# Attention and feed-forward on one core: batch 0's token transpose placed ahead of batch 1's query transpose, and the third w2 block sum moved to VectorE

## Chip, cores and metric

The kernel runs on one core of one Trainium2 chip, in one launch. The metric is the device time of that launch in microseconds (us). Five runs of the kernel before gave 280.51 to 281.52 us, with a median of 280.81 us. One further execution was profiled.

## What is computed

There are 8 batches, 8 heads, 576 positions and 64 features per head. The first half is an attention that never forms a 576 x 576 matrix; the second half is a layer norm and a feed-forward block with a residual:

```
q_s = softmax of q over the 64 features;  k_s = softmax of k over the 576 positions
kv  = einsum('bhsd,bhse->bhde', k_s, v);  attn = einsum('bhsd,bhde->bhse', q_s, kv)
x   = attn as (batch, 576, 512)
out = x + relu(layer_norm(x, g_ln, eps=1e-6) @ w_ch1) @ w_ch2      # w_ch1 512 x 2048, w_ch2 2048 x 512
```

Inputs and output are float32.

## The kernel before

**Tiling.** Of each batch, 512 positions are handled as four tiles of 128; the last 64 positions of all eight batches are collected into a ninth group (`xT8`, `x8`). For every batch the attention result is made with features on the partitions (`xsT`, 128 x 512 in four slices). This is what the first matmul reads. The residual, the statistics of the layer norm and the final additions need it the other way round, with positions on the partitions (`x`). That copy is made by a DMA transpose, `x<-xsT` at L487 in `tokens()`. Four BATCH_NORM_STATS2 (L490) and four aggregates (L491) on VectorE then give the variances, and two small ScalarE operations (L492, L494) the reciprocal deviation `rstd`. Centring is folded into the weights (`centre_w1`), so the first matmul does not wait for the statistics; only the last additions (`ot`, `cp`) do.

**Attention of a batch.** The loads of q, k and v go into staging buffers `stg` (L239, all on SP's queue). ScalarE takes the exponential of q (L326); VectorE sums it (`zq`, L328), takes the reciprocal (`rzq`, L330) and scales (`eq`, L332). A DMA transpose (`eqT<-eq`, L337, in `dma_t()`) turns the scaled queries. ScalarE makes `ek` (L353) and `vb` (L359) from k and v; TensorE forms the 64 x 64 products per head (L370), and VectorE and ScalarE scale them to `kve`. Then TensorE forms `xT` from `eqT` and `kve` (L398; L421 for the last 64 positions), and ScalarE copies it to `xsT` (L411).

**Feed-forward of a batch.** `mm1` runs 16 groups of four matmuls (L538, 128x512), each group evicted with a ReLU to `hT` (L501 on ScalarE; for batch 0 some on VectorE, L503). Batch 0 then uses the plain `mm2` (L681, 64 matmuls of 128x512 into the four `pg` banks). Its four results are evicted at L694, which reads `pg`, `rstd` and `x`. Batches 1 to 7 and the ninth group use `mm2_split`, a product of 2 x 2 blocks with seven block products (L618). It needs sums of blocks of `hT` (`S`, L554) and of `w2` (`T`, L569, made once in `w2_sums`), and evicts through L628. Of the four sums T0 to T3 in `w2_sums`, T2 runs on GpSimd, the others on VectorE; each is made in four pieces of 128x512. The GpSimd pieces read a one-column tile `hold` that GpSimd copies from batch 0's first result `ot` (L754), so they start after it.

**What sets the order.** All work is first entered in a `Plan` as tasks: engine, estimated duration, class, reads, writes, tasks it must follow in order (`after`), and a `slack` that is added to the moment at which it counts as ready. `order()` simulates the engines with these numbers. Whenever an engine is free it takes, of the ready tasks, the one of the lowest class and then of the lowest number. DMAs share one modelled queue; a DMA transpose is entered with 0.9 MB and a landing time, and keeps SP until 0.8 us before its data have passed the queue. `emit()` writes the instructions in that order, so each engine runs a fixed list. When a wait takes longer on the chip than in the plan, everything behind it on that engine waits too.

**Around the change.** Loads are chained through `gate[1]` in the order in which they are entered. The first batch whose attention overlaps feed-forward work is batch 1 (`kind == "early"`). At the end of its loads, after the last load of v, the code enters the query transpose and then the tokens of batch 0:

```
            gate[1] = dma_t()
            state["eqT"] = gate[1], tokens(0, 0.7, (gate[1],))
```

Batch 2's loads follow `state["eqT"]`. Inside `mm2(0)`, the `xT` matmuls of batch 1 may enter TensorE's list after chosen steps (`second_x`, L687). Batch 1's `mm1` reads `xsT` of batch 1, and its first four groups write `pa` banks; the fifth group is the first that needs a `pg` bank released by L694.

Of the kernel before, what the change touches and what calls it, by code (L numbers as in the profile page):

```python
# [12 lines left out]
FP32 = mybir.dt.float32  # L13
# [4 lines left out]
ALU = mybir.AluOpType  # L18
# [116 lines left out]
def dve_t(n, mode=1):  # L135
    return 0.15 + n / (960.0 * mode)
# [3 lines left out]
def kernel(  # L140
# [10 lines left out]
    nc = tc.nc  # L151
# [3 lines left out]
    P = 128  # L155
    J = 4
# [13 lines left out]
    def sb(shape, dt, name):  # L170
        return persist.tile(shape, dt, name=name, tag=name)
# [12 lines left out]
    eq = [sb([P, 2, JT, P], BF16, f"eq{i}") for i in range(2)]  # L184
    eqT = [sb([P, 2 * JT, P], BF16, f"eqT{i}") for i in range(2)]
    kve = [sb([P, G, D], FP16, f"kve{i}") for i in range(2)]
    hold = sb([P, 1], FP32, "hold")
    xb = [sb([P, J, DM], FP16, f"x{i}") for i in range(3)]
    x8 = sb([P, J, DM], FP16, "x8")
    xsT = [sb([P, J * KO1, P], FP16, f"xsT{i}") for i in range(2)]  # L190
# [3 lines left out]
    ot = [sb([P, 2, DM], FP32, f"ot{i}") for i in range(NOT)]  # L194
# [5 lines left out]
    T = [sb([P, HK, 256], FP16, f"T{i}") for i in range(4)]  # L200
# [3 lines left out]
    bst = sb([P, J, 6], FP32, "bst")  # L204
# [6 lines left out]
    plan = Plan()  # L211
# [3 lines left out]
    def nxt(what, n):  # L215
        i = cnt[what] % n
        cnt[what] += 1
        return i
# [17 lines left out]
    gate = [(), None]  # L236
# [72 lines left out]
    def attn(b, kind, between=None, exps=(), sums_=(), kvs=()):  # L309
# [5 lines left out]
        cls = 0 if kind == "first" else 1  # L315
# [20 lines left out]
        def dma_t():  # L336
            return plan.add("SP", 2.2, lambda: nc.sync.dma_start_transpose(  # L337
                eqT[u], eq[u].rearrange("p q j c -> p (q j c)")),
                r=[("eq", u, 0), ("eq", u, 1)], w=EK(u), mb=0.9, land=3.5 if steady else 0.6, after=() if steady else (gate[1],))
# [122 lines left out]
        if steady:  # L462
            state["eqT"] = (dma_t(),)
        else:
            gate[1] = dma_t()
            state["eqT"] = gate[1], tokens(0, 0.7, (gate[1],))
        for hf in range(2):
            keys(hf, lk[hf])
            values(hf, lv[hf])
# [7 lines left out]
    def xof(c):  # L477
        return (xb[c % 3], ("x", c % 3), st[c % 3], ("st", c % 3)) if c < B else (x8, "x8", st[3], ("st", 3))

    def tokens(c, cls=1, after=(), stats=()):  # L480

        x, xk, sti, stk = xof(c)
        if c < B:
            src, r = xsT[c % 2], XK(c % 2)
        else:
            src, r = xT8, [("xT8", b, i) for b in range(B) for i in range(2)]
        i = plan.add("SP", 2.2, lambda: nc.sync.dma_start_transpose(x.rearrange("p j (k c) -> p (j k) c", k=KO1), src.rearrange("p n t -> p (n t)")),  # L487
                 r=r, w=[(xk, j) for j in range(J)], mb=0.9, land=0.6, after=after)
        for j in range(J):
            plan.add("DVE", dve_t(512), lambda j=j: nc.vector.bn_stats(bst[:, j, :], x[:, j, :]), r=[(xk, j)], w=[("bst", j)], cls=cls, slack=2.0 if c else 0.5, after=stats)  # L490
            plan.add("DVE", 0.18, lambda j=j: nc.vector.bn_aggr(bmv[:, j, :], bst[:, j, :]), r=[("bst", j)], w=[("bmv", j)], cls=cls)  # L491
        plan.add("ACT", 0.3, lambda: nc.scalar.activation(sti[:, 3, :], bmv[:, :, 1], AF.Ln, bias=eps, scale=GS * GS),  # L492
                 r=["eps"] + [("bmv", j) for j in range(J)], w=[(stk, "v", j) for j in range(J)], cls=0)
        state["rstd"] = plan.add("ACT", 0.2, lambda: nc.scalar.activation(sti[:, 4, :], sti[:, 3, :], AF.Exp, scale=-0.5),  # L494
                 r=[(stk, "v", j) for j in range(J)], w=[(stk, "r", j) for j in range(J)], cls=0)
        return i


# [58 lines left out]
        tt(3, h12, S[1][:, ks], ALU.subtract, sk(1) + hi)  # L557
        tt(2, h11, h21, ALU.subtract, lo)

    def w2_sums(k0, n, after):  # L560

        ks, kh = slice(k0, k0 + n), slice(HK + k0, HK + k0 + n)
        b11, b12 = w2_sb[:, ks, 0:256], w2_sb[:, ks, 256:512]
        b21, b22 = w2_sb[:, kh, 0:256], w2_sb[:, kh, 256:512]
        lo, hi = [("w2", k0 + i) for i in range(n)], [("w2", HK + k0 + i) for i in range(n)]
        tk = lambda i: [("T", i, k0 + j) for j in range(n)]
        def tt(i, a, b, r):
            eng, e = ("POOL", nc.gpsimd) if i == 2 else ("DVE", nc.vector)
            plan.add(eng, 1.2 if i == 2 else dve_t(256 * n, 2), lambda: e.tensor_tensor(T[i][:, ks], a, b, op=ALU.subtract),  # L569
                     r=r + (["hold"] if i == 2 else []), w=tk(i), cls=2, after=after if i == 2 else ())  # L570
        tt(0, b12, b11, lo)
        tt(1, b22, T[0][:, ks], hi + tk(0))
        tt(2, b22, b12, lo + hi)
        tt(3, b21, T[1][:, ks], hi + tk(1))
# [5 lines left out]
    def store(c, o, hf):  # L580

        if c == B:
            plan.add("SP", 0.62, lambda: nc.sync.dma_start(last_rows(hf), ot[o]), r=[("ot", o, 0), ("ot", o, 1)], mb=0.52, land=2.0, cls=0)
            return
        for e in range(2):
            src = ot[o][R * e : R * e + R]
            plan.add("SP", 0.62, lambda e=e, src=src: nc.sync.dma_start(
                out[c].rearrange("(p j) c -> p j c", j=JT)[:, 4 * hf + e : 4 * hf + e + 3 : 2, :], src),
                r=[("ot", o, 0), ("ot", o, 1)], mb=0.36, land=2.0, cls=0)
# [82 lines left out]
    def mm2(c):  # L672

        gis = [nxt("pg", 4) for _ in range(J)]
        ids = []
        steps = [(8, 1), (8, 3), (12, 1)]
        for k0 in range(0, KO2, 4):
            for j in range(J):
                def f(k0=k0, j=j):
                    for kk in range(k0, k0 + 4):  # L680
                        nc.tensor.matmul(pg[gis[j]], hT[:, kk, j * P : j * P + P], w2_sb[:, kk, :],  # L681
                                         start=(kk == 0), stop=(kk == KO2 - 1))
                i = plan.add("PE", 0.864, f, r=[("hT", kk) for kk in range(k0, k0 + 4)] + [("w2", kk) for kk in range(k0, k0 + 4)], w=[("pg", gis[j])])
                if j == 0:
                    ids.append(i)
                if (k0, j) in steps:
                    second_x(steps.index((k0, j)), (i,))  # L687
        plan.fill(ids[0], ids[-1], zeros(pg[gis[0]], False))
        evs = []
        for hf in range(2):  # L690
            o = nxt("ot", NOT)
            for i in range(2):
                j = 2 * hf + i
                ev = plan.add("DVE", dve_t(512), lambda o=o, i=i, j=j: nc.vector.scalar_tensor_tensor(  # L694
                    ot[o][:, i, :], in0=pg[gis[j]], scalar=st[c % 3][:, 4, j : j + 1], in1=xb[c % 3][:, j, :],
                    op0=ALU.mult, op1=ALU.add),
                    r=[("pg", gis[j]), (("x", c % 3), j), (("st", c % 3), "r", j)], w=[("ot", o, i)], cls=0)
                evs.append(ev)
            store(c, o, hf)
        return evs[:1]  # L700

    def zeros(bank_, start):
        def f(n):
            for _ in range(n):
                nc.tensor.matmul(bank_, zero[:, :P], zero, start=start, stop=start, skip_group_check=True)  # L705
        return f
# [7 lines left out]
    state = {"eqT": (), "ev": [], "stats": ()}  # L714
    opened = [nxt("pg", 4) for _ in range(4)]
    open_ids = []
    def first_w1():
        centre_w1(0)
        open_ids.extend(mm1_open(opened))

    rest = attn(0, "first", first_w1)
    for blk in range(1, 4):
        load_w1(blk)
# [11 lines left out]
    w2_rows(0)  # L735
    w2_rows(4)
    second_x = attn(1, "early", second_w2)

    before = ()
    for b in range(B):  # L740
        if b:
            state["tok"] = tokens(b, 0.7, stats=state["stats"])
        if b == B - 1:
            tokens(8, 0.7, stats=state["stats"])
        ids = mm1(b, b > 0, () if b else opened)
        if b == 0:
            plan.fill(warmed, open_ids[0], zeros(pg[3], True))
            plan.fill(open_ids[-1], ids[0], zeros(pg[opened[0]], False))
        elif b < B - 1:
            attn(b + 1, "steady", None, before, (ids[0],), (ids[10],))  # L750
        before = (ids[-1], state["rstd"])
        if b == 0:
            evs = mm2(b)
            plan.add("POOL", 0.2, lambda: nc.gpsimd.tensor_copy(hold, ot[0][:, 0, :1]), r=[("ot", 0, 0)], w=["hold"])  # L754
            for k0 in range(0, HK, 2):
                w2_sums(k0, 2, evs)
        else:
            mm2_split(b)
    mm1(8, True)
# [37 lines left out]
```

The softmax here doesn't subtract the row's maximum and nothing guards it: scores larger than these inputs give would overflow.

## Time and profile before

| what | value |
|---|---|
| median of five runs (lowest to highest) | 280.81 us (280.51 to 281.52) |
| the profiled execution, its own time | 280.94 us |
| its span in the profile | 279.2 us |
| granted TensorE clock | 1.00 |
| TensorE busy (matmuls) | 271.0 us, 97% of the span |
| VectorE / ScalarE / GpSimd busy | 199.1 / 167.6 / 5.9 us |
| share of the chain that ended last: TensorE, VectorE, DMA, ScalarE | 78%, 13%, 6%, 2% |
| DMA moved | 55.35 MB, mean 198 GB/s |

The profile lists for each group of instructions its line, engine, operation and tile, its busy time, and the idle time of the engine just ahead of it with what ended it. Matmul spans overlap, so a busy TensorE need not be at its peak; its idle stretches are what can be won back. The chain of work that ended last is followed back from the last instruction, at each step to what released it. From about 83.5 us to the last store that chain is almost wholly TensorE; before that it passes through VectorE, DMA and ScalarE as well.

### The profile page before, as it was taken

What the parts mean: (1) busy time and instruction counts of PE and PEld (TensorE: products, weight loads), DVE (VectorE), ACT (ScalarE), POOL (GpSimd) and SP (SyncE); (2) the same over time, 40 slices, a digit from 0 to 9 for tenths busy, and PEclk for the clock granted to TensorE, in tenths of its full rate; (3) what the DMA queues carried; (4) which work ended last, traced back from release to release, by engine and by line L of the source; (5) the groups of instructions that cost most, each with busy time, mean ns of one, the idle gap of its engine ahead of it and who ended that gap; (6) DMA issues with size and microseconds to landing.
All of it is one profiled execution on the core that took longest, in us unless ns stands there. A gap on an engine that the chain in (4) does not pass through costs nothing.

```text
span 279.2 us, 5657 instructions
## 1 busy us (share of the span) xinstructions
PE 271.0 (97%) x2327; PEld 164.5 (59%) x2327; DVE 199.1 (71%) x406; ACT 167.6 (60%) x273; POOL 5.9 (2%) x15
## 2 busy tenths in 40 slices
PE   8999999989799999999999999999999999999994
PEld 2444444436674478447844784478447844874583
DVE  0878896499859967976599569764996773641572
ACT  4668976399468695668566946685655077016500
POOL 1000000060000000000000000000000000000000
PEclk9999999999999999999999999999999999999999
DMA  7999999998977996579858975798543450023004
GB/s 261 363 386 387 387 389 192 270 347 228 337 245 150 220 382 71 150 163 384 124 151 164 392 116 150 160 391 122 153 85 72 81 153 0 0 49 104 0 2 151
DMA packets 57953, 55.35 MB, mean 198 GB/s; under 512 B 36676, under 2 KB 37192, under 8 KB 57928
## 3 DMA queue, kind: packets, MB, share of 16 engines
q1 hardware_dynamic: 57776, 54.86, 69.1%
q8 instruction: 18, 0.29, 0.4%
q10 hardware_dynamic: 152, 0.13, 0.1%
q14 instruction: 7, 0.06, 0.1%
HBM read 36.70 MB, written 9.44 MB: 165 GB/s over the span
## 4 chain that ended last, share of the span: by engine, by line
PE 78%; DVE 13%; DMA 6%; ACT 2%; issue 1%; SPq 0%
PE pg L538 38%; PE pg L618 32%; DMA stg<-in_moe_w_ch_dram 3%; PE pg L705 3%; DVE eq L332 2%; DMA x<-xsT 2%; DVE S L554 2%; DVE zq L328 2%; DVE bst L490 2%; PE pa L370 1%; PE pa L618 1%; DVE T L569 1%; PE pa L398 1%; DVE ot L694 1%; PE pa L282 1%
## 5 line engine op out<-in xcount | busy, mean ns | idle before, releaser
L501 ACT ACTIVATE hT<-pg 128x512 f16<-128x512 f32 x134 | 78.8, 599 | 67.4 <-PE pg L538 67.0
L538 PE MATMUL pg<-xsT,w_sb 128*128 128x512 f16 x488 | 108.3, 379 | 1.0 <-DVE ot L694 0.4
L538 PEld LDWEIGHTS <-w_sb 128*128 128x128 f16 x568 | 54.8, 98 | 66.1 <-issue 1.7
L618 PEld LDWEIGHTS <-S 128*128 128x128 f16 x512 | 49.8, 98 | 7.5 <-issue 1.5
L618 PE MATMUL pg<-T,S 128*128 128x256 f16 x368 | 42.2, 273 | 1.5 <-DVE cp L628 1.5
L618 PEld LDWEIGHTS <-hT 128*128 128x128 f16 x384 | 37.0, 98 | 8.2 <-issue 3.0
L554 DVE TENSOR_TENSOR S<-hT 128x1024 f16<-128x1024 f16 x32 | 21.8, 684 | 24.0 <-ACT hT L501 24.0
L628 DVE SCALAR_TENSOR_TENSOR cp<-pg,st,x 128x256 f32<-128x256 f32 x46 | 20.2, 478 | 13.3 <-PE pg L618 12.6
L618 PE MATMUL pg<-w_sb,hT 128*128 128x256 f16 x248 | 29.4, 273 | 0.0
L490 DVE BATCH_NORM_STATS2 bst<-x 128x6 f32<-128x512 f16 x36 | 24.1, 671 | 7.3 <-DMA x<-xsT 7.2
L628 DVE SCALAR_TENSOR_TENSOR ot<-pg,st,cp 128x256 f32<-128x256 f32 x47 | 20.5, 477 | 11.4 <-PE pg L618 11.3
L332 DVE TENSOR_TENSOR eq<-eq,rzq 128x1152 bf16<-128x1152 bf16 x16 | 22.7, 1418 | 0.5
L328 DVE TENSOR_REDUCE zq<-eq 128x18 f32<-128x1152 bf16 x16 | 21.5, 1344 | 0.3 <-ACT eq L326 0.3
L359 ACT CAST vb<-stg 128x1152 f16<-128x1152 f32 x16 | 18.7, 1167 | 3.8 <-DMA stg<-in_v_dram 3.8
L326 ACT ACTIVATE eq<-stg 128x1152 bf16<-128x1152 f32 x16 | 18.7, 1175 | 2.2 <-DMA stg<-in_q_dram 2.0
L353 ACT ACTIVATE ek<-stg 128x1152 bf16<-128x1152 f32 x16 | 18.7, 1166 | 1.6 <-DMA stg<-in_k_dram 1.5
L411 ACT CAST xsT<-pa 128x512 f16<-128x512 f32 x30 | 15.5, 601 | 3.5 <-PE pa L398 3.5
L705 PE MATMUL pg<-zero 128*128 128x512 f16 x52 | 15.1, 441 | 1.2 <-DVE zero L224 1.2
L618 PE MATMUL pg<-w_sb,S 128*128 128x256 f16 x128 | 15.3, 273 | 0.0
L618 PE MATMUL pg<-T,hT 128*128 128x256 f16 x120 | 14.4, 272 | 0.4 <-DVE ot L628 0.4
L681 PE MATMUL pg<-w_sb,hT 128*128 128x512 f16 x64 | 14.7, 380 | 0.0
L538 PE MATMUL pg<-xT,w_sb 128*128 128x512 f16 x64 | 14.0, 379 | 0.0
(64 smaller groups left out, 164.6 us busy)
## 6 DMA issues: line engine op xcount, KB each, us to landing
stg<-in_q_dram SPq DMA_DIRECT2D x16, 576.0 KB, 5.4
stg<-in_k_dram SPq DMA_DIRECT2D x16, 576.0 KB, 6.9
stg<-in_v_dram SPq DMA_DIRECT2D x16, 576.0 KB, 8.0
out_dram<-ot SPq DMA_DIRECT2D x33, 256.0 KB, 3.5
stg<-in_moe_w_ch_dram SPq DMA_DIRECT2D x16, 512.0 KB, 9.5
out_dram<-ot SPq DMA_DIRECT2D x1, 512.0 KB, 2.8
x<-xsT SPq DMA_TRANSPOSE x8, 6.8
out_dram<-ot SPq DMA_DIRECT2D x1, 128.0 KB, 2.7
```

The costliest lines, as they stand in the source:

```text
L326: plan.add("ACT", act_t(QW), lambda: nc.scalar.activation(e.rearrange("p j (s d) -> p s j d", s=2), sv(s), AF.Exp), r=sk(s), w=[("eq", u, ...
L328: plan.add("DVE", dve_t(QW), lambda: nc.vector.reduce_sum(zq[:, hf], eh, axis=AX.X), r=[("eq", u, hf)], w=[("zq", hf)], cls=qcls, after=sums_)
L332: plan.add("DVE", dve_t(QW), lambda: nc.vector.tensor_tensor(eh, eh, rzq[:, hf].to_broadcast([P, 2 * JT, D]), op=ALU.mult), r=[("rzq", hf) ...
L353: plan.add("ACT", act_t(QW), lambda: nc.scalar.activation(ek[u][:, hf].rearrange("p j (s d) -> p s j d", s=2), sv(s), AF.Exp), r=sk(s), w= ...
L359: plan.add("ACT", act_t(QW), lambda: nc.scalar.copy(vd, va), r=sk(s), w=[("vb", u, hf, i) for i in range(2)], cls=cls, slack=late, after=t ...
L490: plan.add("DVE", dve_t(512), lambda j=j: nc.vector.bn_stats(bst[:, j, :], x[:, j, :]), r=[(xk, j)], w=[("bst", j)], cls=cls, slack=2.0 if ...
L501: nc.scalar.activation(hT[:, m, :], bank, AF.Relu)
L538: nc.tensor.matmul(bank[gi], w1_sb[:, ko, m * P : m * P + P], xt[:, ko], start=(ko == 0), stop=(ko == KO1 - 1))
L554: plan.add("DVE", dve_t(256 * n, 2), lambda: nc.vector.tensor_tensor(S[i][:, ks], a, b, op=op), r=r, w=sk(i), cls=0.3 if k0 else 0.45)
L618: nc.tensor.matmul(g[i][0], fa(k, i), fb(k), start=(first and k == 0 and (i == 0 or g[0][1] != g[1][1])), stop=(last and k == HK - 1), ski ...
L628: nc.vector.scalar_tensor_tensor(dst[:, i, :], in0=g[i][0], scalar=sti[:, 4, 2 * t0 + i : 2 * t0 + i + 1], in1=src[:, i, :], op0=ALU.mult, ...
L705: nc.tensor.matmul(bank_, zero[:, :P], zero, start=start, stop=start, skip_group_check=True)
```

## The change

1. In `attn`, for batch 1, the tokens of batch 0 are entered ahead of the query transpose and follow the last load directly. The query transpose follows them, and `state["eqT"]`, which batch 2's loads follow, holds the query transpose alone.
2. In `tokens`, the slack of the statistics is 2.0 for every batch; it was 0.5 for batch 0.
3. In `w2_sums`, T2 goes to VectorE with the other sums, at class 2 and without the tile `hold`, the GpSimd copy or the wait for batch 0's first result. `mm2` returns nothing.

```diff
-    hold = sb([P, 1], FP32, "hold")
...
         else:
+            gate[1] = tokens(0, 0.7, (gate[1],))
             gate[1] = dma_t()
-            state["eqT"] = gate[1], tokens(0, 0.7, (gate[1],))
+            state["eqT"] = (gate[1],)
...
-            plan.add("DVE", dve_t(512), lambda j=j: nc.vector.bn_stats(bst[:, j, :], x[:, j, :]), r=[(xk, j)], w=[("bst", j)], cls=cls, slack=2.0 if c else 0.5, after=stats)
+            plan.add("DVE", dve_t(512), lambda j=j: nc.vector.bn_stats(bst[:, j, :], x[:, j, :]), r=[(xk, j)], w=[("bst", j)], cls=cls, slack=2.0, after=stats)
...
-    def w2_sums(k0, n, after):
+    def w2_sums(k0, n):
...
         def tt(i, a, b, r):
-            eng, e = ("POOL", nc.gpsimd) if i == 2 else ("DVE", nc.vector)
-            plan.add(eng, 1.2 if i == 2 else dve_t(256 * n, 2), lambda: e.tensor_tensor(T[i][:, ks], a, b, op=ALU.subtract),
-                     r=r + (["hold"] if i == 2 else []), w=tk(i), cls=2, after=after if i == 2 else ())
+            plan.add("DVE", dve_t(256 * n, 2), lambda: nc.vector.tensor_tensor(T[i][:, ks], a, b, op=ALU.subtract),
+                     r=r, w=tk(i), cls=2)
...
         if b == 0:
-            evs = mm2(b)
-            plan.add("POOL", 0.2, lambda: nc.gpsimd.tensor_copy(hold, ot[0][:, 0, :1]), r=[("ot", 0, 0)], w=["hold"])
+            mm2(b)
             for k0 in range(0, HK, 2):
-                w2_sums(k0, 2, evs)
+                w2_sums(k0, 2)
```

More of the change, by code (lines that the diff above doesn't have):

```diff
@@ L494, in tokens @@
         state["rstd"] = plan.add("ACT", 0.2, lambda: nc.scalar.activation(sti[:, 4, :], sti[:, 3, :], AF.Exp, scale=-0.5),
-                 r=[(stk, "v", j) for j in range(J)], w=[(stk, "r", j) for j in range(J)], cls=0)
+                                 r=[(stk, "v", j) for j in range(J)], w=[(stk, "r", j) for j in range(J)], cls=0)
         return i
@@ L688, in mm2 @@
         plan.fill(ids[0], ids[-1], zeros(pg[gis[0]], False))
-        evs = []
         for hf in range(2):
@@ L693, in mm2 @@
                 j = 2 * hf + i
-                ev = plan.add("DVE", dve_t(512), lambda o=o, i=i, j=j: nc.vector.scalar_tensor_tensor(
+                plan.add("DVE", dve_t(512), lambda o=o, i=i, j=j: nc.vector.scalar_tensor_tensor(
                     ot[o][:, i, :], in0=pg[gis[j]], scalar=st[c % 3][:, 4, j : j + 1], in1=xb[c % 3][:, j, :],
@@ L697, in mm2 @@
                     r=[("pg", gis[j]), (("x", c % 3), j), (("st", c % 3), "r", j)], w=[("ot", o, i)], cls=0)
-                evs.append(ev)
             store(c, o, hf)
-        return evs[:1]
     def zeros(bank_, start):
```

## The prediction

> **What bounds the kernel now.** I asked first where TensorE stands idle, because it is busy for 97% of the span. From about 83.5 us on, the chain that ended last is all TensorE, with idle pieces of 0.03 us at most, so the end moves by as much as the start of that stretch moves. The waits of TensorE between 50 and 84 us are four:
>
> ```profile
> engine line waited for: us in total, times, longest us
> PE pg L618 <- DVE cp L628: 1.5, 1, 1.5
> PE pg L538 <- DVE ot L694: 0.4, 1, 0.4
> PE pg L538 <- ACT hT L501: 0.4, 1, 0.4
> PE pg L618 <- DVE ot L628: 0.4, 1, 0.4
> ```
>
> Together 1.50 + 0.43 + 0.42 + 0.41 = 2.76 us. The chain in order of time says what stands behind the first three:
>
> ```profile
> 45.68 5.97 DMA x<-xsT
> 51.65 0.02 issue
> 51.67 0.71 DVE bst L490
> ...
> 55.33 0.21 ACT st L494
> 55.55 0.02 issue
> 55.57 2.73 DVE ot L694 x4
> ...
> 59.89 2.34 DVE eq L332
> ...
> 74.16 0.89 DVE cp L628 x2
> 75.05 0.04 issue
> 75.09 5.42 PE pg L618 x48
> ```
>
> Batch 0's x lands at 51.65. Only then come its statistics, `rstd` and the four evictions `ot` at 55.57. From there VectorE runs without a break until `cp` at 74.16, which TensorE awaits. So VectorE is some us late through batch 1, and the late x is where this begins. ScalarE's 0.42 has the same root: its exponential of batch 2's q comes after L494 in its list (55.71), just ahead of the ReLUs. The fourth wait, 0.41, is another matter: TensorE ends the third block product, and the next one needs the bank that L628 then empties.
>
> Third view, the queue of SP and TensorE's list around it:
>
> ```profile
> 42.30 3.33 SPq L337 DMA_TRANSPOSE eqT<-eq  x1
> 45.68 1.83 SPq L487 DMA_TRANSPOSE x<-xsT  x1
> ```
>
> ```profile
> 47.05 1.04 PE L681 MATMUL pg<-w_sb,hT 128*128 128x512 f16 x4
> 48.02 0.63 PE L398 MATMUL pa<-eqT,kve 64*64 64x512 bf16 x8
> 48.57 1.90 PE L681 MATMUL pg<-w_sb,hT 128*128 128x512 f16 x8
> ```
>
> eqT lands 5.1 us after its issue, at 47.4, and TensorE uses it at 48.02: 0.6 us of room. x, of which the source is ready from about 22 us on, stands behind it.
>
> **What the Trainium skill says.** "DMA: Bandwidth & Descriptors", section "Queues, rings and completion order": each DMA engine takes descriptors in ring order. The trace agrees: x (source long ready) completes only after eqT, at 50.05 against 47.43. The same page, "Why a DMA increments its semaphore by 16 and not by 1": all of up to sixteen engines must report. The trace: fifteen of x's marks come at 49.92 to 50.09, the last at 51.65; a 16 KB instruction fetch (its packet starts at 49.58) lies between data and mark on one engine. "SBUF — State Buffer", "Who interferes with whom": a VectorE operation with two SBUF inputs and a GpSimd one that reads SBUF exclude each other. The trace agrees: GpSimd makes T2 from 56.53 to 61.02, and the L332 in it takes 2.34 us where the others take 1.36. "TensorE: Matmul & The Clock Gate", "Part 1: The HAM clock gate (the "warmup" mystery)": an idle window of about 3.4 us lowers the clock. The wait of 1.50 left it at 1.00, which agrees as far as it goes.
>
> **The change, part by part.**
>
> *T2 to VectorE.* Four instructions of 0.43 us (L569 128x512; seven in a row took 2.80), 1.6 us in all. They join the sums at 42.8 to 45.6 us. VectorE stands idle there and later for 0.19, 0.82 and 3.95 us; that hides them. Without that cover they would cost up to 1.6 us. Their user, the third block product, comes at 75 us. Removed: the GpSimd copy, and 2.34 - 1.36 = 0.98 us of VectorE's chain.
>
> *x ahead of eqT.* x is issued behind the last load of v (issued at 37.54, landed at 44.8), at about 37.9. Five issues of x before (50.54, 101.36, 129.53, 156.67, 185.25) show what a transpose behind loads does: SP is held for 3.8 to 6.3 us, each time until 0.2 to 0.7 us before the last load's landing. One of them:
>
> ```profile
> 101.36 4.24 SPq L487 DMA_TRANSPOSE x<-xsT  x1
> ```
>
> So SP is held to 44.8 - 0.2 = 44.6. Queued behind the held instruction: eqT (ready at 42.27, now 2.3 us later), then batch 2's q loads. x landed 1.6 to 1.8 us after the last load in three of the five (fifteen of its marks in one of them), 3.1 us in two, each with an instruction fetch in its flight: 46.5 to 47.9. I take 46.6, because before no fetch starts between 36 and 49 us. That is 5.0 us earlier than 51.65.
>
> *The statistics.* Four L490 and L491 take 3.3 us from about 48, after batch 1's `kve` on VectorE, and are done by 51.3. ScalarE makes `rstd` behind the four L411 copies. The slack of 2.0 only alters their place in VectorE's list; nothing between 48 and 51.6 competes.
>
> *eqT behind x.* 2304 packets against x's 2048, at the pace of the pair before (eqT 47.43 to x 50.05 is 2.62 us): 2.62 x 2304 / 2048 = 2.95 us behind x, 49.5. To that comes an instruction fetch. TensorE takes one per some 128 matmuls (18 packets of 16 KB for 2327); the one that delayed x at 49.58 comes at the same place in TensorE's list, so now in eqT's flight. Six transposes before met one: the cost was 1.6, 1.5, 1.5, 1.0, 0.65 and 0, mean 1.0. I take the mean: eqT lands at 50.5 (49.3 without a fetch, 51.1 with a late mark).
>
> *Where TensorE waits then.* In the planner's arithmetic a transpose is 0.9 / 0.385 = 2.34 us. Going through its rule by hand, eqT is ready 0.2 us after step (8,3), so one more group of four L681 (0.865 us) goes ahead of L398, the twelve others behind. TensorE reaches L398 at 48.02 + 0.86 = 48.88 and waits until 50.5 + 0.1: **1.7 us lost**. This wait is new. With two groups ahead it would be 0.85, so I keep that for the range. The work behind L398, 12 x 0.216 + 0.2 + 0.55 = 3.3 us, covers the copies to xsT (2.5 us from L398's start at 48.02 to 50.51), so batch 1's `mm1` starts at 52.33 + 1.7 = 54.0.
>
> *What is won back.* `ot` starts behind L398's copies and `rstd`: 50.6 + 2.5 + 0.5 = 53.6, 2.0 earlier than 55.57, while TensorE comes 1.7 later. The fifth group of `mm1` needs `ot` only at 54.0 + 3.5. So 0.43 goes, and 0.42 with it (the exponential ends by about 55.1, as the first ReLU becomes due). At `cp`: TensorE would get there at 73.59 + 1.7 - 0.85 = 74.4. VectorE had 15.1 us from `ot`'s end (58.30) to L491 at 73.38; less 0.98, from 56.3, it is ready at 70.4, or bound by the last ReLU (68.5) with three sums, a statistic, `rstd` and `cp`: 73. So the 1.50 goes. What is late next is TensorE itself. The 0.41 stays: no step touches it. Won: 1.50 + 0.43 + 0.42 = **2.35 us**.
>
> *Other moves.* Batch 2's q loads stand behind both transposes before and after: same bytes ahead, nothing. Batch 0's stores now are ready together with batch 2's loads of k and may go ahead of them, up to 4 x 0.65 = 2.6 us; k was used 3.2 us after it landed (61.65 against 58.48), and ReLUs start later too: nothing, or up to 0.5.
>
> Sum: 1.7 - 2.35 = -0.65. The profiled execution: 280.94 - 0.65 = 280.3; it is 279.2 us of span and 1.7 around it, and stands 0.13 over the median. Against the median: 280.81 - 0.65 = **280.2 us**.
>
> **The rivals.** (1) *The wait only moves.* The fetch falls between eqT's data and its last mark, as it did for x. For: three of six such cases. eqT lands at 51.1, TensorE waits 2.3, sum -0.05: 280.8. Against: the moment of the fetch depends on what is queued. (2) *Slower: eqT becomes the bound of batch 1.* If x, held behind five loads, lands 3.1 us after the last of them, as in two of the five cases, eqT follows at 47.9 + 2.95 = 50.9, and with a late mark at 52.4. TensorE waits 3.6 at L398, sum +1.25: 282.1. It decides from a landing at 51.2 on, where the new wait equals the 2.35. For: the room was 0.6 us only. Against: those two cases had a fetch in them already, and both would have to fall together. The clock gate would add to it only near 3.4 us. (3) *No fetch meets eqT*: lands at 49.5, wait 0.7, sum -1.65: 279.2. One transpose in six that met one lost nothing. I count it to the forecast's case. (4) That the change does nothing cannot be: SP's order fixes which transpose goes first.
>
> **How the numbers follow.** Forecast's case, eqT landing from 49.3 to 50.9 (sum -1.85 to -0.25): 0.55, of which 0.47 below -0.56 us. Rival 1: 0.27. Rival 2: 0.18. A measurement of this kernel tells about 0.2%, 0.56 us, from no change. Faster 0.47, same 0.08 + 0.25 = 0.33, slower 0.18 + 0.02 = 0.20. The range runs from 279.1 (no fetch, or two groups ahead) into rival 2, to 281.4. The forecast's own case is 279.0 to 280.6.
>
> **What would show it.** Right: x issued near 38 with SP held to about 44.6; x landed by 47; T2 on VectorE and each L332 1.36; a new wait of TensorE at L398 of some 1.7 us; `ot` near 53.6; no wait at `cp`. Wrong: a wait at L398 over 2.35, or the wait at `cp` still there.

## The result, and the profile after

The changed kernel takes **283.07 us** (median of 22 runs, 281.31 to 283.51). The kernel before takes 280.82 us in the same comparison. The ratio is 1.006, 95% interval 1.0047 to 1.0072: slower by 2.2 us, where the prediction had 0.6 us faster. The profiled execution has a span of 281.4 us (279.2 before) and a mean granted clock of 0.993 (1.00 before).

The waits of TensorE between 44 and 84 us, after the change:

```profile
engine line waited for: us in total, times, longest us
PE pa L397 <- DMA eqT<-eq: 2.4, 1, 2.4
PE pg L617 <- DVE ot L627: 0.4, 1, 0.4
```

Three of the four waits of before are gone, as forecast, and the 0.4 us at the block product stays. The new wait at `xT` (L397 is L398 of before) is 2.4 us instead of 1.7. The chain in order of time, there:

```profile
43.80 0.98 PE pg L680 x5
44.78 6.50 DMA eqT<-eq
51.28 0.04 issue
51.32 0.63 PE pa L397 x8
51.95 3.37 PE pg L680 x8
55.32 0.25 PE pa L420 x6
```

SP's queue, to set beside 42.30 and 45.68 us of before:

```profile
37.94 6.74 SPq L487 DMA_TRANSPOSE x<-xsT  x1
44.78 2.66 SPq L336 DMA_TRANSPOSE eqT<-eq  x1
```

And TensorE's list; the second number of a line is its length:

```profile
47.03 1.90 PE L680 MATMUL pg<-w_sb,hT 128*128 128x512 f16 x8
51.32 0.63 PE L397 MATMUL pa<-eqT,kve 64*64 64x512 bf16 x8 [2.39 <-DMA eqT<-eq]
51.88 3.44 PE L680 MATMUL pg<-w_sb,hT 128*128 128x512 f16 x8
```

Eight L680 take 1.90 us ahead of the wait and 3.44 us behind it. The table of stretches shows why; it is cut at the moments at which the clock can change (PEclk is the third number from the end):

```profile
core 0: us, PE busy (x) PEld busy (x) DVE busy (x) ACT busy (x) POOL busy (x), PEclk, DMA share, GB/s
48.67:52.08 3.41, 1.02 (x11) 0.36 (x10) 2.76 (x8) 0.32 (x1) 0.00 (x0) 1.00 0.99 308
52.08:55.49 3.41, 3.41 (x16) 1.10 (x14) 1.22 (x2) 2.13 (x6) 0.00 (x0) 0.50 0.27 78
```

After a stretch in which TensorE was busy for 1.02 of 3.41 us, it ran the next 3.41 us at half clock.

These landmarks account for the whole difference (us; `mm1` is a batch's first L538; the tail runs from the start of TensorE's last matmul, which takes 0.27 us, to the end of the span):

| | `mm1` of batch 1 | `mm1` of batch 2 | last matmul starts | span | tail |
|---|---|---|---|---|---|
| before | 52.33 | 83.49 | 275.00 | 279.15 | 4.16 |
| after | 56.37 | 84.69 | 276.02 | 281.39 | 5.38 |

Up to `mm1` of batch 1 the change costs 4.04 us. Before, `mm1` began 4.31 us behind the first `xT` matmul (48.02 to 52.33); with one group of 0.86 moved ahead it would be 3.45. After, it is 5.05 (51.32 to 56.37), so 1.60 us are the half clock, and the other 2.44 the wait. From there to batch 2 the change wins 31.16 - 28.32 = 2.84 us, and another 0.17 us later. The tail grows by 1.22 us. Sum: 2.44 + 1.60 - 2.84 - 0.17 + 1.22 = +2.25; the spans differ by 2.24. Three things are to be explained: why the wait is 2.4 and not 1.7 us, the half clock, and the tail.

The first has its answer in the marks of the DMAs (moments at which the sixteen parts of a transpose were reported, from the trace, us):

```
                  issued   1st to 15th mark   16th mark   TensorE's 16 KB fetch begins
x, before          45.68   49.92 to 50.09     51.65       49.58
eqT, after         44.78   49.41 to 49.55     51.28       49.09
```

Fifteen marks of `eqT` were there by 49.55, where the prediction put its data (49.5); the last is 1.7 us late. An instruction fetch of TensorE begins 0.3 us ahead of the first mark, and its packet ends at 50.08 (0.99 us long), 1.20 us before the late mark. Before, the late mark of `x` came 1.19 us after the end of a fetch (49.58 to 50.46). The late mark has gone from `x` to `eqT`.

### The profile page after: what moved, and what is told of

The parts are those of the page before. It is cut to its first block, busy times and chain, and to the rows that moved or that the text cites. A ratio compares the mean times of both kernels' runs of the same rounds, so it can differ in the third digit from the quotient of the medians.

```text
span 281.4 us, 5654 instructions
## 1 busy us (share of the span) xinstructions
PE 271.1 (96%) x2327; PEld 164.8 (59%) x2327; DVE 199.7 (71%) x410; ACT 169.2 (60%) x273; POOL 1.3 (0%) x10
## 4 chain that ended last, share of the span: by engine, by line
PE 90%; DMA 6%; DVE 1%; ACT 0%; issue 0%; SPq 0%
PE pg L538 42%; PE pg L617 34%; PE pg L680 4%; DMA stg<-in_moe_w_ch_dram 4%; PE pg L701 3%; DMA eqT<-eq 2%; PE pa L369 2%; PE pa L617 1%; PE pa L538 1%; PE pa L397 1%; PE pa L281 1%; DVE ot L627 0%; PE pa L420 0%; DVE zq L327 0%; ACT eq L325 0%
## 5 line engine op out<-in xcount | busy, mean ns | idle before, releaser
L538 PE MATMUL pg<-xsT,w_sb 128*128 128x512 f16 x488 | 108.0, 379 | 1.0 <-DVE w_sb L287 1.0
L538 PEld LDWEIGHTS <-w_sb 128*128 128x128 f16 x568 | 54.9, 98 | 65.5 <-DVE w_sb L287 1.4
L331 DVE TENSOR_TENSOR eq<-eq,rzq 128x1152 bf16<-128x1152 bf16 x16 | 21.7, 1356 | 0.5
L680 PE MATMUL pg<-w_sb,hT 128*128 128x512 f16 x64 | 16.2, 408 | 0.0
L701 PE MATMUL pg<-zero 128*128 128x512 f16 x52 | 13.9, 415 | 1.2 <-DVE zero L223 1.2
L538 PE MATMUL pg<-xT,w_sb 128*128 128x512 f16 x64 | 14.0, 379 | 0.0
```

The source lines that it names most:

```text
L331: plan.add("DVE", dve_t(QW), lambda: nc.vector.tensor_tensor(eh, eh, rzq[:, hf].to_broadcast([P, 2 * JT, D]), op=ALU.mult), r=[("rzq", hf) ...
L538: nc.tensor.matmul(bank[gi], w1_sb[:, ko, m * P : m * P + P], xt[:, ko], start=(ko == 0), stop=(ko == KO1 - 1))
```

## The experiments

The theory after this reading, A: order and sums do what they should, the late mark makes the wait, the wait in an unlucky place makes the half clock, and a late mark of the last store makes the tail. Rivals: the wait itself is the cost and the clock no more than a symptom; or the earlier order is bad in itself (R2, `eqT` bound by the queue even without a late mark).

### Each part alone

`e3_sums_only` is the kernel before with T2 on VectorE (part 3 of the change; cut to its main lines):

```diff
-            eng, e = ("POOL", nc.gpsimd) if i == 2 else ("DVE", nc.vector)
-            plan.add(eng, 1.2 if i == 2 else dve_t(256 * n, 2), lambda: e.tensor_tensor(T[i][:, ks], a, b, op=ALU.subtract),
...
+            plan.add("DVE", dve_t(256 * n, 2), lambda: nc.vector.tensor_tensor(T[i][:, ks], a, b, op=ALU.subtract),
...
```

> The kernel before with the third w2 sum on VectorE only (no hold, no GpSimd sums); x still behind eqT. Theory A: x lands at 51.6 as before, the scaling of batch 2's q takes 1.36 us and not 2.34, so the wait at cp falls from 1.5 to some 0.5 us: 279.9 us. Rival (the sums burden VectorE and carry part of the loss): 280.8 or slower.

Measured: 280.22 us (279.67 to 280.85, 15 runs), ratio 0.9978 (0.9967 to 0.9989). TensorE's waits between 44 and 84 us in it:

```profile
PE pg L616 <- DVE cp L626: 0.6, 1, 0.6
PE pg L537 <- ACT hT L500: 0.4, 1, 0.4
PE pg L616 <- DVE ot L626: 0.4, 1, 0.4
```

The 1.5 us at `cp` are down to 0.6, and the stretch from `mm1` of batch 1 to that of batch 2 from 31.16 to 29.69. This half of the change is a gain.

`e4_order_only` is the kernel before with the new order, T2 still on GpSimd:

```diff
+            gate[1] = tokens(0, 0.7, (gate[1],))
             gate[1] = dma_t()
-            state["eqT"] = gate[1], tokens(0, 0.7, (gate[1],))
+            state["eqT"] = (gate[1],)
```

> The kernel before with only the order changed (batch 0's x ahead of batch 1's query transpose), the third w2 sum still on GpSimd behind the first result. Theory A: the whole loss is here: a wait of 2.4 us for eqT, half clock behind it in most runs, 283 us. Rival (the order alone is harmless, the sums on VectorE make the loss): 280.8 us.

Measured: 281.80 us (280.57 to 282.98, 22 runs), ratio 1.0027 (1.0016 to 1.0039); slower, by less than expected. The wait is the same as with both parts:

```profile
PE pa L398 <- DMA eqT<-eq: 2.3, 1, 2.3
PE pa L421 <- ACT xsT L411: 1.3, 1, 1.3
```

The marks of `eqT` are at 49.41 to 49.55 and the last at 51.22, the fetch begins at 49.14. The stretch to batch 2 is 29.70, so each part alone wins 1.47 us there and both together 2.84.

Of the two parts only the order loses when it stands alone, 0.9 us by the medians; the sums win 0.7. Together they lose 2.2, so about 2.1 us come only with both. One piece is the tail: 4.24 us with the order alone and 4.39 with the sums alone, against 5.38 with both. The other is the half clock: 14 of the 22 runs of `e4_order_only` have a clock of 0.993 or 0.994, but their median is 281.9 us against 281.7 for the other eight, while the same two groups of the changed kernel lie 1.8 us apart (below). The one execution of `e4_order_only` with a trace has no half clock there, so why it costs so little with T2 on GpSimd is not shown.

### The wait against the clock

`e1_busy_wait` is the changed kernel with eleven zero matmuls between the L680 and the `xT` matmuls, so that TensorE works while it would wait:

```diff
+                if kind == "early" and hs[0] == 0:
+                    zeros(state["zb"], False)(11)
...
+        state["zb"] = pg[gis[0]]
```

> The changed kernel with eleven matmuls of zeros (11 x 0.216 = 2.4 us) in TensorE's list ahead of batch 1's xT, so that TensorE works through the new wait of 2.4 us; nothing else moves. Theory A (the wait itself is paid back by the waits it removes; the loss is the clock that drops after it, and a late mark of the last store): no stretch of half clock, the eight matmuls behind xT take 1.9 us and not 3.44, and the time is 281.3 us in all runs, 1.7 under the 283.1 of the changed kernel. Rival R (the clock drop is a by-product of no cost, the wait for eqT alone makes the kernel slower): the time stays near 283.

Measured: 282.42 us (281.50 to 282.77, 6 runs), ratio 1.0054 (1.0035 to 1.0073). The clock was 0.997 to 1.0 in all six runs. TensorE's list there:

```profile
49.27 2.54 PE L704 MATMUL pg<-zero 128*128 128x512 f16 x11
51.74 0.63 PE L399 MATMUL pa<-eqT,kve 64*64 64x512 bf16 x8
52.30 1.90 PE L683 MATMUL pg<-w_sb,hT 128*128 128x512 f16 x8
```

`eqT` is as late as before (last mark 51.58), yet the eight L683 take 1.90 us: a busy TensorE keeps the clock, the idle one loses it. The time fell by 0.65 us only, against 1.8 expected, so by its time alone the run does not decide between the two. Its profiled execution reaches the second eight L540 (L538 of before) at 24.91 us where the changed kernel reached them at 24.41, and it has the same late tail, 5.33 us; the rest is open.

That a wait of this length drops the clock only in some places is seen in `e8_last_store` below. It has nearly the same wait (2.63 us, L397 at 51.38, the last mark of `eqT` at 51.34) and no half clock there. Its stretches, cut at its own boundaries:

```profile
47.08:50.50 3.42, 1.67 (x8) 0.69 (x7) 3.28 (x10) 0.31 (x1) 0.00 (x0) 1.00 1.05 204
50.50:53.91 3.41, 2.53 (x24) 0.98 (x23) 0.83 (x4) 2.09 (x5) 0.00 (x0) 1.00 0.69 270
```

The wait lies across the boundary at 50.50, so that TensorE is busy for 1.67 and 2.53 us of the two. The clock changes on record lie whole numbers of 3.413 us apart: in the changed kernel at 4.29, 52.08 (14 of them later), 55.49 (1) and 280.77 us (66). In `e8_last_store` the first is at 6.12, so the boundaries lie differently in each execution. This fits the two groups into which the runs of the changed kernel fall: 14 of 22 at 282.99 to 283.51 us with a clock of 0.991 to 0.995, and 8 at 281.31 to 282.34 with 0.998 to 1.0. Their medians are 283.25 and 281.46, 1.8 us apart; this, more than `e1_busy_wait`, says what the half clock costs. One stretch at half clock is 0.994 by arithmetic (1 - 0.5 x 3.41 / 280).

`e2_fetch_moved` is the changed kernel with 96 small matmuls (32 x 4) behind the twelve zero matmuls of the start, to shift TensorE's fetches:

```diff
-        return plan.add("PE", 0.43 * n, lambda: zeros(pg[3], True)(n), r=["zero"], w=[("pg", 3)], cls=0)
+        return plan.add("PE", 0.43 * n, lambda: (zeros(pg[3], True)(n), tiny(96)), r=["zero"], w=[("pg", 3)], cls=0)
...
```

> The changed kernel with 96 tiny matmuls (32 x 4) at the end of the first warm-up, so that TensorE reaches the place of each instruction fetch 96 matmuls earlier in its list; no fetch should then lie between eqT's data and its marks. Theory A (one of eqT's sixteen marks is late because of the fetch): all marks of eqT by 49.6 us, the wait of TensorE falls from 2.4 to 0.8 us, the clock stays full, and the time is 280.8 - 0.3 - 1.6 = 278.9 us, or up to 280.0 with a late mark of the last store. Rival R2 (eqT is late because it stands behind x, whatever is fetched): its last mark stays near 51.3 and the time near 283.

Measured: 283.84 us (282.51 to 285.21, 6 runs), ratio 1.0107 (1.0080 to 1.0134). It tells nothing on the time: behind the small matmuls the clock was at half from 9.31 to 12.72 us, and the work behind them came 3.6 us later. On the mark it tells something: the fetch came at 42.37, all sixteen marks of `eqT` at 50.31 to 50.47 (4.6 us after its issue), and TensorE did not wait at `xT`.

### The fetch, moved without that flaw

Each zero matmul of 512 columns is cut into three of 176, 176 and 160, with the same work in all: 104 more matmuls with their weight loads on TensorE, early in its list, so that its later fetches fall elsewhere.

```diff
-                nc.tensor.matmul(bank_, zero[:, :P], zero, start=start, stop=start, skip_group_check=True)
+                for c0, c1 in ((0, 176), (176, 352), (352, 512)):
+                    nc.tensor.matmul(bank_[:, c0:c1], zero[:, :P], zero[:, c0:c1], start=start, stop=start, skip_group_check=True)
```

On the changed kernel, `e6_split_after`:

> The changed kernel with each 512-column matmul of zeros of the warm-up cut into three (176, 176 and 160 columns): the same zeros and the same time on TensorE, 104 matmuls more in its list ahead of batch 1, so each instruction fetch of TensorE comes 104 matmuls earlier in the work. Theory A (a fetch between eqT's data and its marks makes one of sixteen marks late): all marks of eqT by 49.6 us, TensorE's wait at xT falls from 2.4 to 0.8 us, too short to drop the clock; 281.3 - 1.7 = 279.6 us in all runs (with the late mark of the last store still there). Rival R2 (eqT is late because it stands behind x): the last mark stays at 51.3, the wait at 2.4, and the time near 283.

Measured: **280.45 us** (279.39 to 281.79, 22 runs), ratio 0.9980 (0.9969 to 0.9992). TensorE's list:

```profile
47.40 1.90 PE L680 MATMUL pg<-w_sb,hT 128*128 128x512 f16 x8
49.66 0.63 PE L397 MATMUL pa<-eqT,kve 64*64 64x512 bf16 x8 [0.36 <-DMA eqT<-eq]
50.22 1.90 PE L680 MATMUL pg<-w_sb,hT 128*128 128x512 f16 x8
```

The fetches now begin at 37.97 and 53.19, the sixteen marks are at 49.45 to 49.62, the wait is 0.36 us, and there is no half clock there. The same order that cost 2.2 us is now a gain: R2, which said 283, falls. A said 279.6, with the late tail (5.34 us here) already in it, so 0.85 us are missing. In the profiled execution `mm1` of batch 6 comes 28.59 us behind that of batch 5, 0.73 more than in the changed kernel, with a wait of 0.4 us for VectorE's evictions; whether that holds for the median is not shown.

On the kernel before, `e9_split_before`, as a control, and on the sums alone, `e7_split_sums`:

> The kernel before, with the zeros cut in three and nothing else: the control of the other two. Theory A: x lands whole at 50.1 and not at 51.65, the chain to cp starts 1.5 us earlier and the wait of 1.5 there nearly goes: 279.5 us. Rival (the late mark has another cause than the fetch): 280.9.

> The kernel before (x behind eqT) with the third w2 sum on VectorE and the zeros cut in three. Theory A: no fetch lies in x's flight, x lands whole at 50.1 and not at 51.3, so VectorE's chain starts 1.2 us earlier and the waits behind it shrink to the one before the last block product: batch 1's first matmul at 52.4, batch 2's 28.4 us later, and 278.6 us. Rival (the rest of the waits has another cause than x): as the sums alone, 280.2.

Measured: 280.69 us (279.98 to 282.03, 22 runs), ratio 0.9987 (0.9977 to 0.9998), and 279.89 us (278.93 to 281.95, 22 runs), ratio 0.9962 (0.9948 to 0.9976). The cut alone gains 0.13%, so it is not what turned 283.07 into 280.45. Both miss their expectation by more than 1 us. In the profiled control `x` is whole at 50.10 us instead of 51.65, and `mm1` of batch 2 starts 1.55 us earlier; but then TensorE waits for VectorE's evictions behind 84 us, which it never did before:

```profile
PE pg L538 <- DVE ot L628: 1.9, 4, 0.7
```

That execution was the slowest of its 22, so the 1.9 us are its own; `e6_split_after` and `e7_split_sums` show one such wait of 0.4. In these executions what is won ahead of 84 us is in part given back, because VectorE is then the later one. How much of both misses this explains in the medians is open.

### The tail

The last store is issued by ScalarE about 0.8 us after the last matmul starts. Its marks, with the 8 KB instruction fetch nearest to them (us):

```
                   issued    1st mark   15th     16th     fetch begins   tail
before             275.82    277.85     277.99   278.06   277.60         4.16
after              276.84    278.84     279.00   280.13   278.78         5.38
```

`e8_last_store` is the changed kernel with that store on SP:

```diff
-            eng, en = (("SP", nc.sync), ("ACT", nc.scalar))[i]
+            eng, en = "SP", nc.sync
```

> The changed kernel with its very last store issued by SP and not by ScalarE. Theory A (1.1 us of the loss lie behind TensorE's end: an instruction fetch falls ahead of the last mark of the last store): the fetch no longer meets that mark, the time from TensorE's last matmul to the end falls from 5.4 to 4.2 us, and the time is 1.1 us under the changed kernel, 282.0 where the clock drops and 280.2 where it doesn't. Rival (the longer end belongs to the store itself): it stays at 5.4 us or grows, 283.

Measured: 282.46 us (280.60 to 284.32, 22 runs), ratio 1.0038 (1.0021 to 1.0055). The tail of the profiled execution is 4.83 us; the last mark is still late (278.28, the others at 277.34 to 277.47). Half an effect, and the other queue does not avoid it. In the eight executions with a trace in which the last mark of the last store is over 0.8 us late, it comes 1.03 to 1.13 us after the end of an 8 KB fetch; the late mark of the transpose came 1.09 to 1.21 us after the end of a 16 KB one in all six (`x` in the kernel before, `eqT` in five others).

Whose fetch is it? Two runs put eight one-column copies near the start of ScalarE's list, on `e6_split_after` and on the changed kernel:

```diff
+        ...; plan.add("ACT", 0.0, lambda: [nc.scalar.copy(tiny, zero[:, :1]) for _ in range(8)], r=["zero"], w=["tiny"], cls=-1)
```

> The kernel with the zero matmuls cut in three (280.45 us), with eight one-column copies added to ScalarE's list near its start; every other engine's list is unchanged. Theory A says that the late last store is an instruction fetch of ScalarE's own, which starts 0.1 us before the store's marks because ScalarE's list ends one recorded operation short of where it ended before the change; eight more operations bring that fetch forward by several operations, the last mark comes with the other fifteen, the stretch from TensorE's last matmul to the end of the span falls from 5.3 to 4.2 us, and the median is near 279.4 us. Rival B says that the fetch belongs to another engine, or that its moment follows the end of the kernel and not a count of instructions: the tail stays at 5.3 us and the median within 0.4 of 280.4.

> The changed kernel alone with the same eight copies on ScalarE. Theory A: the tail falls from 5.4 to 4.2 us, while the wait for eqT and the half clock stay: median near 281.9 us (283.07 less 1.2). Rival B: tail 5.3 us, median within 0.4 of 283.1.

Measured: 280.26 us (279.32 to 281.40, 22 runs), ratio 0.9981 (0.9970 to 0.9992), tail 5.17; and 282.87 us (281.02 to 282.99, 6 runs), ratio 1.0063 (1.0042 to 1.0085), tail 5.16. This theory A (ScalarE's fetch) falls here. Another 8 KB fetch moved, from behind the end to 260 us; the one near the store stayed 0.09 us ahead of its first mark. `e11b_scalar8` also repeats the main finding: five of its six runs have a clock of 0.991 to 0.994, and the sixth, at 281.02 us, 0.999.

Two more put the eight copies behind the last operation of ScalarE and of VectorE, on `e6_split_after`. This is the one on VectorE (`done` is the last store):

```diff
...
+            if i == 1:
+                plan.add("DVE", 0.1, lambda: [nc.vector.tensor_copy(tiny, zero[:, :1]) for _ in range(8)], r=["zero", ("ot", o2, 0, slots)], w=["tiny"], after=(done,), cls=9)
```

> The kernel with the zero matmuls cut in three, with eight one-column copies on ScalarE behind its last operation, the last store; nothing else moves. The copies take some 0.5 to 0.8 us on an engine that is done by then. Theory C: the 8 KB fetch near the last store is the one that ScalarE makes when it goes from the end of its list to the common end of the program, so it now starts 0.5 us or more later, behind the store's marks; the last mark comes with the others, the tail falls from 5.3 to about 4.3 us and the median to 279.4. Rival D: the fetch is another engine's; it stays 0.1 us ahead of the marks, the tail at 5.2 to 5.3, the median within 0.4 of 280.4.

> The same with the eight copies on VectorE, behind its last addition. Theory D, VectorE's fetch: it starts later by 0.5 us or more, the tail falls to about 4.3 us and the median to 279.4. Theory C, ScalarE's: nothing moves, tail 5.2 to 5.3 us, median within 0.4 of 280.4. If neither run moves the fetch, its owner is SP or TensorE, which ended half a us earlier.

Measured on ScalarE: 279.93 us (279.44 to 280.38, 7 runs), ratio 0.9963 (0.9950 to 0.9976), tail 5.22, last mark 277.50 against 276.20 to 276.59: nothing freed. By itself this says little, since the fetch that lay behind the end is gone and two 8 KB fetches now begin just ahead of these marks (276.06 and 276.14). On VectorE: **279.18 us** (278.82 to 279.92, 6 runs), ratio 0.9943 (0.9928 to 0.9957), the fastest of all. Its tail is 4.26 and its sixteen marks are at 275.89 to 276.07. The fetch is VectorE's: with eight instructions more in that list it comes at 270.36, five us ahead of the marks (it was expected to move later, not earlier), and the one behind the end stays. Beside the same runs of the kernel before, the copies on ScalarE gave 279.93 and those on VectorE 279.18, so 0.75 us by the medians are the mark's (0.96 by the two tails). TensorE's list of this kernel at the place in question:

```profile
47.09 1.90 PE L682 MATMUL pg<-w_sb,hT 128*128 128x512 f16 x8
49.29 0.63 PE L397 MATMUL pa<-eqT,kve 64*64 64x512 bf16 x8 [0.31 <-DMA eqT<-eq]
49.85 1.90 PE L682 MATMUL pg<-w_sb,hT 128*128 128x512 f16 x8
```

So the changed kernel's tasks, with TensorE's and VectorE's instruction fetches moved off two DMA marks, take 279.18 us and not 283.07. The prediction's third rival (no fetch meets `eqT`) said 279.2. That this agrees so well is luck in part: it had a wait of 0.7 us and a gain of 2.35, where 0.31 and 2.84 were measured, and the cut's own 0.13% is in the 279.18.

## Why the prediction was wrong, step by step

**Right: the queue.** SP is held until 44.68 (44.6 forecast), `x` lands at 46.65 (46.6), the data of `eqT` at 49.5 (49.5). One more group of L680 goes ahead of L397.

**Right: the sums on VectorE.** The twelve old and four new pieces take 0.41 us each and delay nobody; every scaling of q is now as fast as the others were:

```profile
L331 DVE TENSOR_TENSOR eq<-eq,rzq 128x1152 bf16<-128x1152 bf16 x16 | 21.7, 1356 | 0.5
L568 DVE TENSOR_TENSOR T<-w_sb 128x512 f16<-128x512 f16 x8 | 3.1, 413 | 0.0
L568 DVE TENSOR_TENSOR T<-w_sb,T 128x512 f16<-128x512 f16 x8 | 3.1, 415 | 0.0
```

This agrees with what the prediction took from the Trainium skill's "SBUF — State Buffer", "Who interferes with whom": without GpSimd beside it, no L331 is longer than the rest. `e3_sums_only` shows the gain alone, 0.7 us by the medians.

**Right: the statistics and the waits behind them.** They ran from 47.6 to 50.9 (done by 51.3 forecast). `ot` came at 54.27 (53.6), late by what `xT` was late. The waits of 1.50, 0.43 and 0.42 are gone, and 0.41 stays.

**Wrong: "I take the mean: eqT lands at 50.5."** This is the step that failed first. The six earlier cases gave 0 to 1.6 us, and their mean of 1.0 is a value that `eqT` showed in none of the ten traces with the new order. With a fetch beginning 0.27 to 0.32 us ahead of the first mark, the sixteenth was 1.57 to 1.73 us behind the fifteenth (five traces: the changed kernel, the order alone, the busy wait, `e8_last_store`, `e11b_scalar8`); with the fetch out of the way, 0.03 to 0.07 us (the other five). So `eqT` landed at 51.28, and the wait was 2.44 us and not 1.7. It was a question of two cases, and there was a reason for one of them: the fetch had begun at 49.58, 0.34 us ahead of `x`'s first mark, and the prediction put the data of `eqT` at 49.5, in the same place. Rival 1 had this mechanism and the right landing (51.1); it got 0.27, and it had no half clock and no tail either.

**Wrong: "Won: 1.50 + 0.43 + 0.42 = 2.35 us."** The waits went, but each was worth more than its idle time. That time is counted from the modelled end of the matmul before it, and in a dense row that end lies behind the next start. From start to start, the waits listed as 0.43, 0.42 and 1.50 had held up what follows by 0.59, 0.58 and 1.68: these are the steps by which the two kernels' lists come closer there. Their sum is 2.85, and 2.84 was won. The new wait, listed as 2.39, costs 2.44.

**Wrong: "The clock gate would add to it only near 3.4 us."** It added 1.60 us at a wait of 2.4 in the profiled execution, and 14 of 22 runs show the clock that goes with it. The prediction leaned on the Trainium skill, "TensorE: Matmul & The Clock Gate", "Part 1: The HAM clock gate (the "warmup" mystery)", for an idle stretch of about 3.4 us. The same section calls the stretch free-running, and the boundaries of this trace agree (3.41 us apart). What differs is the amount of idleness: 1.02 us of work in the stretch did not save the clock, with 1.67 in `e8_last_store` it stayed. The measurement decides: the case has to be priced for a wait of 2.4 us too, with a chance for its place.

**Wrong: "the end moves by as much as the start of that stretch moves."** It holds for TensorE's last matmul within 0.17 us. It does not hold for the end of the kernel: the last store's sixteenth mark became 1.1 us late. No part of the prediction looked at the tail. Neither part of the change makes this mark 1.1 us late alone (tails 4.24 and 4.39 us); with both, VectorE's fetch begins 0.06 us ahead of the first mark instead of 0.25. `e13_end_vector` shows that eight more instructions in VectorE's list are enough to take the fetch away and the mark back.

By terms: predicted -0.65; wait 2.44 instead of 1.7 (+0.74), half clock +1.60, gain 2.84 and not 2.35 (-0.49), later -0.17, tail +1.22. That gives +2.25. The largest term, the half clock, and the tail were at nothing in the prediction. Rival 2 came nearest in time (282.1) for a wrong reason: `x` wasn't late and the landing was not 52.4.

**Left open.** Why with both parts the fetch of VectorE comes later against the marks than in the kernel before (mostly 0.06 to 0.12 us ahead of the first instead of 0.25), why 0.25 does no harm, and why the last mark in `e8_last_store` is late with the fetch 0.5 us ahead. For TensorE's fetches nearness alone does not decide either: in `e9_split_before` one begins 0.08 us ahead of `x`'s first mark and no mark is late, and in the kernel before one begins 0.43 us ahead of the first mark of a later `eqT` (94.74) and the last is 0.07 us late. How a fetch holds a mark back is not shown: the traces do not say which of the sixteen DMA engines carried it.

## What to carry to other kernels

A DMA whose user has under 2 us of room is priced with its last mark, in two cases and not with a mean. Whether an instruction fetch meets it depends on the instruction lists: here 104 more matmuls with the same work in all moved TensorE's fetch, and eight tiny copies moved VectorE's. A wait of TensorE is measured from start to start, and from some 2 us on (an estimate from the busy times 1.02, 1.22 and 1.67 us of 3.41 below) it is priced with the half clock that can follow. Two parts that are tried alone need not add up to the two together. If a sound change comes out slower, look at what its list lengths have shifted before giving it up: here the same tasks are 0.6% slower, or with both lists lengthened 0.6% faster (0.13% of it the cut's own).

## What the runs showed of the hardware that was not expected

- Clock: a wait of 2.4 us was followed by 3.41 us at half clock when it lay within one of the repeating 3.41-us stretches (busy 1.02 us of it), and one of 2.6 us was not when it lay across two (1.67 and 2.53 us busy). Behind the last matmuls of `e4_order_only` a stretch with 1.22 us busy (275.23 to 278.64) is followed by half clock too, so in these traces the limit lies between 1.22 and 1.67 us. An estimate agrees: 41 of the 66 runs of the changed kernel, `e4_order_only` and `e8_last_store` show the lower clock (0.991 to 0.995), and of all placings of a wait of 2.5 us some 60% leave under 1.5 us of work in one stretch.
- Small matmuls (32 x 4, 96 of them) did not hold the clock: half from 9.31 to 12.72 us in `e2_fetch_moved`, though the trace counts TensorE as busy for all of the stretch before (5.89 to 9.31).
- One late mark in sixteen costs a transpose 1.7 us (49.55 to 51.28) with a fetch of 16 KB whose packet took 0.99 us, and the last store 1.1 us with a fetch of 8 KB of 0.31 us. The late mark comes 1.0 to 1.2 us after the end of that packet, in all fourteen cases looked at.
- Eight copies of one column at the end of VectorE's list made `e6_split_after` faster: its ratio to the kernel before was 0.9980 without them and 0.9943 with them, and 0.9963 with the same copies at the end of ScalarE's list.
